# The last four quads of an attention block as 256 tokens of two heads each, with half of the last feed-forward moved forward

## The chip, the cores and the metric

One core of a Trainium2 chip runs the whole kernel. The metric is device time in microseconds of one execution, the median over runs; the profile is that of one execution. Five engines work side by side, each through its own queue in order: PE (TensorE, matrix products into PSUM), ACT (ScalarE), DVE (VectorE), POOL (GpSimd) and SP (SyncE, which here issues transfers). PSUM has eight banks of 128 x 512 floats.

## What is computed

A transformer block over 2048 tokens of width 512, with 32 heads of 16 and a feed-forward of width 1376. Six vectors sa, ca, ga, sb, cb, gb come from one conditioning vector:

```python
h = _layernorm(x, axis=-1) * (1 + ca) + sa
x = x + ga * _A_ref(h, A_wqkv, A_wo)
h = _layernorm(x, axis=-1) * (1 + cb) + sb
x = x + gb * _B_ref(h, B_w1, B_b1, B_w2, B_b2)
```

`_A_ref` is softmax attention with an output projection, `_B_ref` two matrix products with a GELU (tanh form) between them and biases. Inputs and outputs are bf16.

## The kernel before

**Tiling.** Queries go in four blocks `b` of 512 tokens (`NQB`), keys in sixteen tiles `kt` of 128 (`NKT`). Heads go in groups `ch` of eight; within a group the heads lie in pairs on four strips of 32 partitions, so that four heads of the same parity `par` are worked at once. Four heads, 512 queries and all keys are a *quad*; there are 32 (`NQ`), in the order of `divmod(qi, 8)`: block, group, parity (`bt`, L802). I count them from 0 to 31.

**A quad.** For each key tile and strip PE makes scores `S = kT.T qm` (L871, 32 x 128 weights, 512 columns, one of four row groups of the array). Most are turned into weights by ACT: one exponential (L1216) takes the scores of two strips, 1024 columns. The others go another way, "D": DVE rounds score plus constant into int16 (L1287), whose bits read as f16 are a power of two, and makes, with POOL, three shifted copies (L1258 on DVE, L1264 on POOL), which with scaled values `VV` approximate the exponential. PE then multiplies the weights by the values (L1027): 128 x 32 weights, 512 columns, four column groups of the array at once, one for each head. Each head's 32 output rows hold its 16 sums and, from a column of ones, the softmax denominator. All of a quad add up in one bank, which is opened by `open_o`.

**After a quad.** `o_copy` copies the bank to SBUF (L1321, DVE). SP then carries the four rows of denominators to DRAM and back into a 128 x 16 shape (`d`, `dall`, L1331 and L1340), DVE takes reciprocals (L1357), SP writes them out (L1365) and reads them back, repeated over 16 partitions (`rb`, L1375). For the odd quad the rows are merged into those of the even one (L1327). POOL multiplies (L1386) and leaves `OT[(b, ch)]`, 128 channels by 512 tokens. Quad 30 is a special one: its `OT` is made alone, and quad 31 is handled in the tail.

**Feed-forward of a block.** When a block's four `OT` are there, `add_tail(b)` gives jobs: x1 (projection by `W_o` and the residual), norm, transposes by DMA on SP, eleven "u" jobs (up-projection), one GELU on ACT over the whole, four "out" jobs. They are worked between the matmuls of the next block's quads.

**What sets the order.** A program written in Python (from L700) plans everything before the kernel runs: it keeps four clocks, picks at each step the next instruction of PE, ACT, DVE or POOL, and emits it. So the queues are fixed in advance. A job or a task has a gate (a place in the sequence of quads), things it depends on, and a planned duration: `MM` for a step on PE, `K_GATE`, `U_GATE`, `OUT_GATE` and so on for gates. When PE would be idle, `fill` adds four matmuls of zeros (L1042).

**The tail** (`last_tail`, from L1501). Once the loop is over, the sums of quad 31 lie in PSUM. x1 of the last block is nearly done by "z" jobs (residual and three groups, by 128 x 128 matmuls at L680). Then: copy (L1518), the denominators through `pick` (L1522), reciprocal (L1524), spread to rows (L1527, L1529), product (L1533), the last group's part of x1 with `W_z`, statistics (L1562), root on POOL (`ln_root`), the norm's scaling half on DVE and half on ACT (L1573, L1571), transposes on PE (L1580), the up-projection in slices of 256 tokens (`up_one`: four matmuls and a GELU, L1553), ten warming matmuls before it (`warm`, L251), the down-projection (L680), the residual sum and the store. All 512 tokens go through this chain after the loop.

Of the kernel before, what the change touches and what calls it, by code (L numbers as in the profile page):

```python
# [100 lines left out]
Z_AHEAD = 3  # L101
# [3 lines left out]
Z_GATE = 0.2  # L105
# [50 lines left out]
def adaln_block(ctx: ExitStack, tc: tile.TileContext, A_x, A_wqkv, A_wo, B_x, B_w1, B_b1, B_w2, B_b2,  # L156
# [254 lines left out]
    pick = const.tile([P, 4], FP32, name="pick")  # L411
    nc.vector.tensor_copy(out=pick, in_=ident32.rearrange("p (r e) -> p r e", e=32)[:, :, 14])
# [284 lines left out]
    def add_tail(b):  # L697
        X = {}
        def span(g, i, n):
# [3 lines left out]
             lambda: X.update(tail_tiles(b)), out=(SP_X, 512.0))  # L703
# [29 lines left out]

        for fc in range(NFC):
            job(("u", b, fc), span(U_GATE, fc, NFC), [("t2", b, t) for t in range(4)] + [("w1s", j) for j in range(NC)] + [("b1t", 2)],
                [lambda ps, j=j, fc=fc: up_mm(bank(ps), X["h2"], fc, j, mm=mm4) for j in range(NC)],
                [((DV,), lambda eng, ps, fc=fc: u_evac(ps, fc))])
        task(("g", b), span(U_GATE, NFC, NFC), [("u", b, fc) for fc in range(NFC)], AC, 7.5,
# [13 lines left out]
        for tt in range(4):  # L752
            job(("out", b, tt), span(OUT_GATE, tt, 4), [("g", b)] + [("w2g", fc) for fc in range(NFC)],
                [lambda ps, tt=tt, fc=fc: down_mm(bank(ps), X["u"], tt, fc, mm=mm4) for fc in range(NFC)],
                [((DV,), lambda eng, ps, tt=tt: o_evac(ps, tt))])
# [4 lines left out]

    def outer(ps, tt):
        b, cs = NQB - 1, slice(tt * P, (tt + 1) * P)
        return [lambda: plain(ps, ident, XL["xr"][:, tt, :], True, False)] + [
            lambda ch=ch: plain(ps, OT[(b, ch)][:, cs], W_o[:, ch, :], False, False) for ch in range(3)]

    for tt in range(Z_AHEAD):
        job(("z", tt), NQ - Z_GATE + 0.001 * tt, ["xlast"] + [("ot", NQB - 1, ch) for ch in range(3)],
            [lambda ps, tt=tt, i=i: outer(bank(ps), tt)[i]() for i in range(4)], [], mode="full")
    task("xlast", 8 * NQB - 0.9, [("out", NQB - 2, tt) for tt in range(4)], "SP", 0.0,
         lambda: XL.update(tail_tiles(NQB - 1)), out=(SP_X, 512.0))  # L770
# [30 lines left out]

    def bt(qi):  # L802
        b, t = divmod(qi, 8)
# [65 lines left out]
    def qk(dst, qi, kt, r):  # L869
        b, ch, par = bt(qi)  # L870
        nc.tensor.matmul(out=dst, lhsT=kT[32 * r:32 * r + 32, ch, kt * P:(kt + 1) * P],  # L871
                         rhs=qm[(b, ch)][32 * r:32 * r + 32, par, :], start=True, stop=True)
# [114 lines left out]
    def open_o(now):  # L987
        qi = opened[0]
        if qi < NQ and may_open(qi) and o_wait(now):
            f = flex_free(now)  # L990
            if f:
# [4 lines left out]
                left_q[qi] = 4  # L996

# [18 lines left out]
    def pv_issue(now, sel):  # L1016
        s = pe_start(now, "col", MM, "col" if len(sel) == 4 else f"part{len(sel)}")
        for r, e in sel:
# [3 lines left out]
            h = 8 * ch + 2 * r + par  # L1022
            lo = VOFF + HS * h - (16 if par else 0)
            w = VE[:, kt, lo:lo + 32] if not j else VV[:, DKT.index(kt), j - 1, lo:lo + 32]
            n = emitted[qi][r] + 1
            last = total(qi) == n
            nc.tensor.matmul(out=bank(O[qi])[32 * r:32 * r + 32, :], lhsT=w, rhs=rhs, start=(n == 1), stop=last)  # L1027
# [8 lines left out]
    def fill(now):  # L1036
        for qi in sorted(O):
            rs = [r for r in range(4) if emitted[qi][r] and emitted[qi][r] != total(qi)]
            if len(rs) == 4:
                pe_start(now, "col", MM, "fill")  # L1040
                for r in rs:
                    nc.tensor.matmul(out=bank(O[qi])[32 * r:32 * r + 32, :], lhsT=zeros[:, 0:32],  # L1042
                                     rhs=hT[:, r, 0:512], start=False, stop=False)
# [48 lines left out]
    def pe(now):  # L1092
        if issue_unit(now):
            return True
        open_o(now)
# [81 lines left out]
    def do_task(now, e, upto=INF):  # L1177
        p = min(pos(), upto)
        for tk in tasks:
            if tk.gate > p:  # L1180
                break
            if tk.eng == e and is_done(tk.deps, now):
                if e == "SP" and tk.name[0] in ("tb", "xlast") and now < chain[0]:
# [118 lines left out]
    def o_copy(now):  # L1302
        if not o_done or o_done[0][0] > now:
            return False
        if bt(o_done[0][1])[2] and o_done[0][1] < NQ - 1 and o1_free[0] > now:
            return False
# [5 lines left out]
        if par == 0:  # L1312
# [10 lines left out]
        row = 14 if par else 16  # L1323
        d1 = scr.tile([4, 512], FP32, name="d1")

        def merge(r):
            nc.sync.dma_start(out=o[32 * r + 16:32 * r + 32, :], in_=dst[32 * r + 16:32 * r + 32, :])  # L1327
            return dma(st["ev"], SP_O)

        def first():  # L1330
            nc.sync.dma_start(out=d1, in_=dst.rearrange("(r e) n -> r e n", e=32)[:, row, :])  # L1331
            land = dma(t, SP_D)
            st["ev"] = t
            if par:
                for r in range(2):
                    merge(r)
            at(land, lambda: second(land))

        def second(now):
# [3 lines left out]
            if par:  # L1343
# [5 lines left out]
        if par:  # L1349
# [11 lines left out]
        def after(now, rp):  # L1361
# [7 lines left out]
            def bq(now):  # L1369
                for r in range(4):  # L1370
                    lo = 32 * r + 16 * par
                    if qi == NQ - 2:
                        nc.sync.dma_start(out=rb[32 * r:32 * r + 32, :], in_=d2[r:r + 1, :].to_broadcast([32, 512]))
                    else:
                        nc.sync.dma_start(out=rb[lo:lo + 16, :], in_=d2[r:r + 1, :].to_broadcast([16, 512]))  # L1375
                    land = dma(now, SP_RB)
                chain[0] = land
                if par or qi == NQ - 2:
                    done[("rb", b, ch)] = land + DMA_SLACK

            at(now, a)
            if par or qi == NQ - 2:
                def mk():
                    ot = otp.tile([P, 512], BF16, name="OT")
                    OT[(b, ch)] = ot
                    nc.gpsimd.tensor_tensor(out=ot, in0=o, in1=rb, op=ALU.mult)  # L1386

                tasks.insert(0, Task(("ot", b, ch), -1, [("rb", b, ch)], PO, 1.42, mk))
# [62 lines left out]
    while more_units() or bulk or filled or dbanks or dcur[0] or shifts or any(queue) or O or len(jobs) or xopen or evacs:  # L1451
# [34 lines left out]
        else:  # L1486
            T[e] = now + 0.02
            guard += 1
            if guard > 40000:
# [12 lines left out]
    def last_tail():  # L1502
# [5 lines left out]
        rest = [i for i in range(8) if i != kO and i not in pz]  # L1508
        po, kw, kd, kr = pz + rest[0:4 - len(pz)], *rest[4 - len(pz):7 - len(pz)]
# [3 lines left out]
        rx = odp.tile([P, 512], FP32, name="rb")  # L1513

        def last_ch(tt):
            plain(bank(po[tt]), OT[(b, 3)][:, tt * P:(tt + 1) * P], W_z[:, 0, :], False, False)

        nc.vector.tensor_copy(out=o, in_=bank(kO))  # L1518
        for tt in range(len(pz)):
            last_ch(tt)  # L1520
        for tt in range(4):
            nc.tensor.matmul(out=bank(kd)[:, 4 * tt:4 * tt + 4], lhsT=o[:, tt * P:(tt + 1) * P], rhs=pick,  # L1522
                             start=True, stop=True)
        nc.vector.reciprocal(out=rt.rearrange("p t r -> p (t r)"), in_=bank(kd)[:, 0:16])  # L1524
        for tt in range(4):
            cs = slice(tt * P, (tt + 1) * P)
            nc.vector.tensor_copy(out=rx[:, cs].rearrange("p (r e) -> p r e", e=32),  # L1527
                                  in_=rt[:, tt, :].unsqueeze(2).to_broadcast([P, 4, 32]))
            nc.tensor.matmul(out=bank(kr)[:, cs], lhsT=rx[:, cs], rhs=ident32, start=True, stop=True)  # L1529
        nc.scalar.activation(out=onec, in_=onec, func=ACT.Gelu_apprx_tanh)  # L1530
        for h in range(2):
            cs = slice(256 * h, 256 * h + 256)
            nc.vector.tensor_tensor(out=otl[:, cs], in0=o[:, cs], in1=bank(kr)[:, cs], op=ALU.mult)  # L1533
        nc.sync.dma_start(out=scr_d1, in_=o.rearrange("(r e) n -> r e n", e=32)[:, 14, :])
        nc.sync.dma_start(out=dall[:, NQ - 1, :], in_=scr_d1.rearrange("r (p f) -> (r p) f", f=16))
        def last_par(tt):
            plain(bank(po[tt]), otl[:, tt * P:(tt + 1) * P], W_z[:, 1, :], False, True)

        for tt in range(2):
            last_par(tt)  # L1540
        for tt in range(len(pz), 4):
            for fn in outer(bank(po[tt]), tt):
                fn()
            last_ch(tt)
        for tt in range(2, 4):
            last_par(tt)
        warm(10, kw)

        def up_one(fc, cs, k):
            ps = bank(k)[:, 0:256]  # L1550
            for j in range(NC):
                up_mm(ps, h2, fc, j, cs)
# [214 lines left out]
```

## Time and profile before

| | |
|---|---|
| median of 3 runs | 757.46 us (756.5 to 757.7) |
| the profiled execution | 757.77 us, span of its trace 756.0 us |
| granted TensorE clock | 0.997 |
| exponentials, L1216 | 734 |
| score matmuls, L871 | 2048, of which 580 feed DVE's way |
| value matmuls, L1027 | 3788, in 947 groups of four |
| last scores of quad 31 begin | 719.31 us |
| the sums of quad 31 are copied | 721.59 us |
| first up-projection of the last block | 732.38 us |
| last down-projection ends | 752.53 us |

In the timeline a line is a run of like instructions: start, us, engine, line of the code, operation, output and inputs, shape, number, and in brackets how long the engine was idle before and who released it. In the table of groups the columns are busy time and mean length, and then the idle time before them. `32*128` is the part of the array that a matmul uses, rows by columns.

### The profile page before, as it was taken

Reading aid. Unit: us, or ns where it says so; the run is one execution under the profiler, and the core shown is the slowest. Engines: PE = TensorE matmul, PEld = TensorE weight load, DVE = VectorE, ACT = ScalarE, POOL = GpSimd, SP = SyncE. Lnnn points to the kernel's source line nnn. Section 1 sums busy time; section 2 is a strip of 40 time slices with the busy share of each in tenths; the row PEclk is TensorE's granted clock in tenths of the full one; section 3 lists DMA queues with packets and bytes.
Section 4 is the critical chain, followed back from the end, with each engine's and each line's share of the span. In section 5 each row is a group of like instructions: output and inputs, shape, how many; then the busy total and the mean of one; then the engine's idle time right before and its main releaser. Section 6 shows DMA issues by size and latency. Waiting matters only on the chain.

```text
span 756.0 us, 21028 instructions
## 1 busy us (share of the span) xinstructions
PE 738.0 (98%) x8528; PEld 229.1 (30%) x8528; DVE 686.2 (91%) x1196; ACT 720.7 (95%) x778; POOL 420.5 (56%) x264
## 2 busy tenths in 40 slices
PE   7999999999999999999999999999999999999998
PEld 3322322222233222222232222222222222222255
DVE  5958999999989999999999999999999999999942
ACT  3999999999999999999999999999999999999953
POOL 3202557666566753276659575765666656657510
PEclk9999999999999999999999999999999999999999
DMA  8410100021210110000100200001010200001100
GB/s 297 130 22 2 25 11 17 8 67 48 59 50 11 26 28 13 14 17 24 45 17 10 43 7 16 10 23 24 28 34 3 45 10 17 10 17 31 42 12 31
DMA packets 40248, 25.33 MB, mean 34 GB/s; under 512 B 25265, under 2 KB 34962, under 8 KB 40146
## 3 DMA queue, kind: packets, MB, share of 16 engines
q1 hardware_dynamic: 39186, 22.69, 11.7%
q8 instruction: 68, 1.11, 0.6%
q10 hardware_dynamic: 960, 1.25, 0.5%
q14 instruction: 34, 0.28, 0.1%
HBM read 16.72 MB, written 2.61 MB: 26 GB/s over the span
## 4 chain that ended last, share of the span: by engine, by line
ACT 49%; PE 37%; issue 8%; DVE 3%; POOL 2%; DMA 0%; POOLq 0%; DVEq 0%; ACTq 0%
ACT pB L1216 23%; ACT pA L1216 23%; PE PS L1027 13%; PE PS L871 12%; PE PS L246 7%; PE PS L680 3%; POOL t L1264 2%; ACT uG L739 1%; DVE t L1287 1%; PE PS L1042 1%; DVE t L1258 1%; DMA xb<-in_A_x_dram 0%; PE PS L251 0%; ACT L1216 0%; DVE st L273 0%
## 5 line engine op out<-in xcount | busy, mean ns | idle before, releaser
L1264 POOL TENSOR_SCALAR t<-t 128x2048 int16<-128x2048 int16 x189 | 358.0, 1901 | 250.9 <-DVE t L1258 130.1
L1216 ACT ACTIVATE pA<-PS 128x1024 bf16<-128x1024 f32 x367 | 391.8, 1068 | 3.7 <-PE PS L871 3.6
L1287 DVE TENSOR_SCALAR t<-PS 128x512 int16<-128x512 f32 x580 | 374.8, 680 | 21.5 <-PE PS L871 18.5
L1216 ACT ACTIVATE pB<-PS 128x1024 bf16<-128x1024 f32 x367 | 391.7, 1067 | 0.4 <-PE PS L871 0.2
L871 PE MATMUL PS<-qm,kT 32*128 32x512 bf16 x2048 | 308.2, 383 | 5.6 <-ACT pB L1216 1.9
L1027 PE MATMUL PS<-t,VV 128*32 128x512 f16 x1740 | 225.5, 385 | 3.2 <-POOL t L1264 2.7
L1258 DVE TENSOR_SCALAR t<-t 128x2048 int16<-128x2048 int16 x246 | 177.0, 743 | 0.4
L871 PEld LDWEIGHTS <-kT 32*128 32x128 bf16 x2048 | 85.6, 91 | 298.0 <-issue 295.3
L1027 PE MATMUL PS<-pA,VE 128*32 128x512 bf16 x734 | 166.8, 385 | 0.0
L1027 PE MATMUL PS<-pB,VE 128*32 128x512 bf16 x734 | 164.1, 386 | 0.0
L1027 PE MATMUL PS<-t,VE 128*32 128x512 f16 x580 | 141.8, 385 | 0.2 <-DVE t L1287 0.2
L1027 PEld LDWEIGHTS <-VE 128*32 128x32 bf16 x2048 | 61.8, 94 | 75.4 <-issue 68.8
L1027 PEld LDWEIGHTS <-VV 128*32 128x32 bf16 x1740 | 58.0, 94 | 64.2 <-issue 57.9
L246 PE MATMUL PS<-h2T,W 128*32 128x512 bf16 x528 | 42.6, 383 | 0.0
L246 PE MATMUL PS<-W,uG 128*32 128x512 bf16 x528 | 40.7, 383 | 0.0
L1386 POOL TENSOR_TENSOR OT<-o_sb,rb 128x512 bf16<-128x512 f32 x16 | 20.4, 1274 | 14.7 <-DVE t L1258 6.8
L1042 PE MATMUL PS<-hT,zeros 128*32 128x512 bf16 x284 | 28.3, 382 | 0.0
L731 DVE TENSOR_SCALAR uG<-PS,b1c 128x512 bf16<-128x512 f32 x33 | 24.5, 741 | 1.5 <-PE PS L246 1.5
L333 DVE TENSOR_SCALAR qm<-PS,qmask 128x512 bf16<-128x512 f32 x32 | 22.6, 741 | 3.5 <-PE PS L246 3.3
L283 POOL TENSOR_SCALAR rs<-mv 128x4 f32<-128x4 f32 (+1 forms) x10 | 4.5, 449 | 32.3 <-DVE mv L278 31.8
L246 PE MATMUL PS<-hT,W_k 128*32 128x512 bf16 x256 | 21.3, 398 | 0.9 <-DVE hT L316 0.9
L246 PE MATMUL PS<-hT,W_q 128*32 128x512 bf16 x256 | 21.3, 397 | 0.0
(133 smaller groups left out, 381.7 us busy)
## 6 DMA issues: line engine op xcount, KB each, us to landing
rb<-d SPq DMA_DIRECT2D x120, 32.0 KB
W_m<-in_w_mod_dram SPq DMA_DIRECT2D x2, 1024.0 KB
xr<-in_A_x_dram SPq DMA_DIRECT2D x4, 512.0 KB
o_sb<-o SPq DMA_DIRECT2D x60, 32.0 KB
out_dram<-ob SPq DMA_DIRECT2D x14, 128.0 KB
xb<-in_A_x_dram SPq DMA_DIRECT2D x3, 512.0 KB
W<-in_B_w_dram SPq DMA_DIRECT2D x4, 344.0 KB
W<-in_B_w_dram SPq DMA_DIRECT2D x5, 256.0 KB
```

The costliest lines, as they stand in the source:

```text
L246: nc.tensor.matmul(out=ps[32 * g:32 * g + 32, :], lhsT=lhsT[:, 32 * g:32 * g + 32], rhs=rhs, start=start, stop=stop)
L333: nc.vector.tensor_scalar(out=qm[(b, ch)][:, par, :], in0=ps, scalar1=qmask[:, par:par + 1], scalar2=None, op0=ALU.mult)
L680: nc.tensor.matmul(out=ps, lhsT=lhsT, rhs=rhs, start=start, stop=stop)
L731: nc.vector.tensor_scalar(out=X["u"][:, fc, :], in0=bank(ps), scalar1=late["b1c"][:, fc:fc + 1], scalar2=None, op0=ALU.add)
L871: nc.tensor.matmul(out=dst, lhsT=kT[32 * r:32 * r + 32, ch, kt * P:(kt + 1) * P], rhs=qm[(b, ch)][32 * r:32 * r + 32, par, :], start=True, ...
L1027: nc.tensor.matmul(out=bank(O[qi])[32 * r:32 * r + 32, :], lhsT=w, rhs=rhs, start=(n == 1), stop=last)
L1042: nc.tensor.matmul(out=bank(O[qi])[32 * r:32 * r + 32, :], lhsT=zeros[:, 0:32], rhs=hT[:, r, 0:512], start=False, stop=False)
L1216: nc.scalar.activation(out=t[:, 0:n, :], in_=PS[:, b0:b0 + n, :], func=ACT.Exp, scale=math.log(2.0) / STEP)
L1258: nc.vector.tensor_scalar(out=t16[:, rs, :], in0=d["tile"][:, rs, :], scalar1=float(MJ[j]), scalar2=None, op0=ALU.add)
L1264: nc.gpsimd.tensor_scalar(out=t16[:, rs, :], in0=d["tile"][:, rs, :], scalar1=1.0, scalar2=float(MJ[j]), op0=ALU.mult, op1=ALU.add)
L1287: nc.vector.tensor_scalar(out=d["tile"][:, r:r + n, :], in0=PS[:, i:i + n, :], scalar1=T_BIAS, scalar2=0.0, op0=ALU.add, op1=ALU.max)
L1386: nc.gpsimd.tensor_tensor(out=ot, in0=o, in1=rb, op=ALU.mult)
```

## The change

Six things are changed.

1. The last four quads are cut otherwise. They are still those of block 3, groups 2 and 3, but each now holds 256 tokens of *both* parities: quad 28 is group 2, first half; 29 group 3, first half; 30 and 31 the second half. A score matmul still has 512 columns (two parities of 256). A value matmul becomes two of 256 columns, one for each parity, with different weights into the same strip. The bank is opened by four matmuls of zeros.
2. `o_copy` follows: two transfers of denominators in place of one, four merges within the quad's own tile, eight broadcasts of 256, and an `OT` of 256 tokens for each of these quads but the last.
3. x1, statistics and norm of the *first* 256 tokens of the last block become jobs and tasks of the loop (`add_half`, gate `XA_AT`), with the norm's scaling on POOL and the transposes by DMA. They lie in parts of `hT` that nothing reads any more (`xa`, `ha`, `ua`); filler matmuls read `kT` for that reason, and the path for out-of-range inputs, which is not run with these inputs, computes again what it took from `hT`.
4. In the tail only the second 256 tokens go through the chain. The first half's up- and down-projection are steps of a generator, and `gap(n)` issues n of them at six places of the chain (`GAPS`). The ten warming matmuls go.
5. "z" jobs, now two, are for the second half alone; the x load is in two parts.
6. Gates: `K_GATE`, `U_GATE`, `OUT_GATE`, `Z_GATE`, `OPEN_N`, and own ones for block 2.

The core of the diff:

```diff
-K_GATE = (-1.7, 0.25)
+K_GATE = (-1.7, 0.22)
-U_GATE = (1.7, 5.0)
-OUT_GATE = (4.6, 7.8)
-OPEN_N = 14
+U_GATE = (2.2, 5.2)
+OUT_GATE = (5.0, 7.9)
+OPEN_N = 12
-Z_AHEAD = 3
+GAPS = (4, 2, 2, 17, 2, 3)
+NHQ = 4
+N2_ENG = PO
+NHC = NC - NHQ // 2
+MMH = 0.25
+XA_AT = 30.5
+U2_GATE = (1.7, 4.6)
+OUT2_GATE = (4.6, 7.2)
-Z_GATE = 0.2
+Z_GATE = 0.6
...
+    def halved(qi):
+        return qi >= NQ - NHQ
+
     def bt(qi):
+        if halved(qi):
+            h, n = divmod(qi - NQ + NHQ, NHQ // 2)
+            return NQB - 1, NHC + n, h
...
+                if halved(qi):
+                    pe_start(now, "col", MM, "opens")
+                    for r in range(4):
+                        nc.tensor.matmul(out=bank(f[0])[32 * r:32 * r + 32, :], lhsT=zeros[:, 0:32], rhs=zeros,
+                                         start=True, stop=False)
+                    return True
...
         for r, e in sel:
...
+            for pr in range(2) if halved(qi) else (par,):
+                lo = VOFF + HS * (8 * ch + 2 * r + pr) - (16 if pr else 0)
+                w = VE[:, kt, lo:lo + 32] if not j else VV[:, DKT.index(kt), j - 1, lo:lo + 32]
+                cs = slice(256 * pr, 256 * pr + 256) if halved(qi) else slice(0, 512)
+                nc.tensor.matmul(out=bank(O[qi])[32 * r:32 * r + 32, cs], lhsT=w, rhs=rhs[:, cs],
+                                 start=(n == 1 and not halved(qi)),
+                                 stop=last and (pr == 1 or not halved(qi)))
...
+        for tt in range(2):
+            job(("xA", tt), XA_AT, ["xl0"] + [ot_key(ch, 0) for ch in range(NC)],
+                [lambda ps, tt=tt, ch=ch: mm4(bank(ps), ot_cols(ch, tt), W_o[:, ch, :], ch == 0, ch == NC - 1)
+                 for ch in range(NC)],
+                [((DV,), lambda eng, ps, tt=tt: x1(ps, tt))])
+            task(("s2", b, tt), XA_AT, [("xA", tt)], DV, 0.64, lambda tt=tt: ln_stats(xa, XL["st"], tt))
+        task(("a2", b), XA_AT, [("s2", b, tt) for tt in range(2)], DV, 0.3,
+             lambda: XL.update(mv=ln_aggr(XL["st"][:, 0:2, :], 2)))
+        task(("r2", b), XA_AT, [("a2", b)], PO, 1.2, lambda: XL.update(rs=ln_root(XL["mv"], 2)))
+        def n2(tt):
+            hn.append(otp.tile([P, 512], BF16, name="OT"))
+            eng = nc.vector if N2_ENG == DV else nc.gpsimd
+            eng.tensor_scalar(out=hn[tt], in0=xa[:, tt, :], scalar1=XL["mv"][:, tt, 0:1],
+                                    scalar2=XL["rs"][:, tt:tt + 1], op0=ALU.subtract, op1=ALU.mult)
+        for tt in range(2):
+            task(("n2", b, tt), XA_AT, [("r2", b)] + [("n2", b, 0)] * tt, N2_ENG, 0.36 if N2_ENG == DV else 0.55,
+                 lambda tt=tt: n2(tt))
+            task(("t2", b, tt), XA_AT, [("n2", b, tt)], "SP", 0.0,
+                 lambda t=tt: transpose_dma(ha[:, :, t * P:(t + 1) * P], hn[t]), out=(SP_T, 0.0))
...
+                for r in range(4):
+                    for i in range(2) if half else (par,):
+                        lo = 32 * r + 16 * i
+                        nc.sync.dma_start(out=rb[lo:lo + 16, 0:w], in_=d2[r:r + 1, cs].to_broadcast([16, w]))
...
+        def fillers():
+            for fc in range(NFC):
+                up_one(fc, (kw, dA[1])[fc % 2], 0)
+                for _ in range(2):
+                    yield
+            for tt in range(2):
+                for fc in range(NFC):
+                    plain(bank(dA[tt]), ua(fc)[:, tt * P:(tt + 1) * P], late["W_2"][:, fc, :], fc == 0, fc == NFC - 1)
+                    yield
...
         nc.vector.tensor_copy(out=o, in_=bank(kO))
+        nc.scalar.activation(out=onec, in_=onec, func=ACT.Gelu_apprx_tanh)
+        gap(GAPS[0])
...
-        warm(10, kw)
```

The tail after that goes on: `pick` (four matmuls), reciprocal, `gap(2)`, the spread to rows, `gap(2)`, the two products and the last parts of x1 of two token tiles, statistics and root, `gap(17)`, the norm's scaling (one tile on ACT, one on DVE), transposes, `gap(2)`, four slices of the second half's up-projection, the rest of the generator, seven more slices, the flag, and the down-projection of the second half.

More of the change, by code (lines that the diff above doesn't have):

```diff
@@ L1513, in last_tail, with up_one @@
         rx = odp.tile([P, 512], FP32, name="rb")
[L1515 to L1522, printed above, removed]
+        hA, hB = slice(0, 256), slice(256, 512)
+        obs = {}
+        def up_one(fc, k, half):
+            ps = bank(k)[:, 0:256]
+            for j in range(NC):
+                up_mm(ps, h2 if half else ha, fc, j, hB if half else hA)
+            nc.scalar.activation(out=uG[:, fc, hB] if half else ua(fc), in_=ps, func=ACT.Gelu_apprx_tanh, bias=b1c[:, fc:fc + 1],
+                                 scale=1.0)
```

290 lines of the change are left out of this document (160 added, 130 removed).

## The prediction

> **What bounds the kernel now.** I read the page first: busy shares and the chain of waits.
>
> ```profile
> PE 738.0 (98%) x8528; PEld 229.1 (30%) x8528; DVE 686.2 (91%) x1196; ACT 720.7 (95%) x778; POOL 420.5 (56%) x264
> ACT 49%; PE 37%; issue 8%; DVE 3%; POOL 2%; DMA 0%; POOLq 0%; DVEq 0%; ACTq 0%
> L1216 ACT ACTIVATE pA<-PS 128x1024 bf16<-128x1024 f32 x367 | 391.8, 1068 | 3.7 <-PE PS L871 3.6
> ```
>
> Up to 721 us the exponentials (L1216) and TensorE set the time together: ACT carries 49% of the chain, PE 37%. Exponentials start 0.907 us apart when nothing holds them (the 1068 ns of a row overlap). Second, the timeline of the last 40 us:
>
> ```profile
> 719.31 0.39 PE L871 MATMUL PS<-qm,kT 32*128 32x512 bf16 x2
> 720.07 0.38 PE L1027 MATMUL PS<-pB,VE 128*32 128x512 bf16 x2
> 720.28 0.60 PE L1027 MATMUL PS<-t,VV 128*32 128x512 f16 x8
> 721.59 0.69 DVE L1518 COPY o_sb<-PS 128x512 f32<-128x512 f32 x1 [2.31 <-PE PS L1027]
> 723.64 0.95 PE L1522 MATMUL PS<-pick,o_sb 128*128 128x4 f32 x8
> 732.38 3.22 PE L680 MATMUL PS<-h2T,W 128*128 128x256 bf16 x28 [0.45 <-ACT h2T L324]
> 742.62 7.30 PE L680 MATMUL PS<-W,uG 128*128 128x512 bf16 x33
> 752.57 0.37 ACT L324 CAST ob<-PS 128x256 bf16<-128x256 f32 x1 [9.47 <-PE PS L680]
> ```
>
> The last scores start at 719.31, the last quad's sums are copied at 721.59, and until 732.38, 10.8 us, PE mostly waits for a chain of small steps (denominators, x1, norm, transposes). Then 20.2 us of dense feed-forward run to 752.53; the span ends at 756.0. The change wants to put half of that feed-forward into the 10.8 us. Third, what its input would have to come through: the chain of the last but one quad ("quad 30"), DVE and then everything, and two POOL rows:
>
> ```profile
> 705.26 0.68 DVE L1321 COPY o_sb<-PS 128x512 f32<-128x512 f32 x1
> 707.29 1.87 DVE L1287 TENSOR_SCALAR t<-PS 128x512 int16<-128x512 f32 x3
> ```
> ```profile
> 714.90 0.23 DVE L1357 RECIPROCAL rp<-dall 128x16 f32<-128x16 f32 x1
> 715.17 0.32 SPq L1365 DMA_DIRECT2D d<-rp  x1
> 716.20 3.08 DVE L1258 TENSOR_SCALAR t<-t 128x2048 int16<-128x2048 int16 x5
> 716.61 2.61 SPq L1373 DMA_DIRECT2D rb<-d  x4
> 721.09 1.27 POOL L1386 TENSOR_TENSOR OT<-o_sb,rb 128x512 bf16<-128x512 f32 x1 [6.44 <-DMA rb<-d]
> ```
> ```profile
> L1264 POOL TENSOR_SCALAR t<-t 128x2048 int16<-128x2048 int16 x189 | 358.0, 1901 | 250.9 <-DVE t L1258 130.1 <-PE PS L871 39.3 <-DVE t L1287 27.4
> L577 POOL TENSOR_SCALAR W_z<-W_o,pmask 128x512 bf16<-128x512 bf16 x2 | 3.1, 1574 | 0.6 <-DVE o_sb L1321 0.6
> ```
>
> From its copy to its scaled output quad 30 takes 705.26 to 722.36, longer than the loop still runs.
>
> **The change, part by part**, against this execution (span 756.0, its own time 757.77; the median of the runs is 757.46).
>
> (1) *The loop, amounts.* By the two built programs' orders there are 736 exponentials for 734, 576 passes L1287 for 580, 244 DVE shifts for 246, 71 filler groups in both. For PE I price every step of the order by starts in this trace: 0.2175 us for a group of four 128x32 matmuls (720.07 to 720.28, and on), 0.314 where the array changes between row and column tiles, 0.2175 for a 128x128 one. That gives 667.6 before. The last four quads now take their 124 value groups as eight 256-wide matmuls. No row shows such a group; 256-wide matmuls at L680 stand 0.112 apart (6.71 for 60), so two per column group in turn are 0.224 from below. From above: if the eight ran column after column, four steps of 0.107, 0.43. I take 0.23, because in this trace a matmul of a free column group does not wait for one whose column is busy:
>
> ```profile
> 240.47 0.39 PE L1027 MATMUL PS<-pA,VE 128*32 128x512 bf16 x2
> 240.48 0.59 PE L246 MATMUL PS<-W_o,OT 128*32 128x512 bf16 x4
> ```
>
> The pair at 240.47 holds column groups 0 and 1. Of the four behind it two start 0.01 later and two at 240.69; the records at 240.69 are those with the wait on DVE, which the program gives to the first of the four. So groups 2 and 3 went first. With 0.23 PE's price is 667.8 (three groups more for x1, four zero openings, fewer tile changes elsewhere): +0.2. ACT's is two exponentials, 2 x 0.907 = +1.8. Both bind in turn, so the loop's end moves by +0.2 to +1.8; I take +0.6, nearer PE, whose order loses fewer steps in the quads before. With 0.43 per group PE's price is +25.
>
> [...]
>
> (2) *Quad 30's chain and the first half's norm.* This sets my end. Take as zero the scores of the exponential before which the last two passes ahead of quad 30's copy are fed; 15 exponentials follow, so the last scores stand at 15 x 0.93 = 13.95 (0.93 is the pace of these quads with their small waits: 23 in 21.4 us in quad 31). DVE then has: pass, copy, two more passes, an x1 add and a stats, three passes, a shift (passes 0.60 apart, 707.29) and reaches the reciprocal at 6.8. From there by the rows above: 0.27 to d, 1.44 to rb, eight broadcasts instead of four at 0.43 (1.72 for four of 16 rows) 3.44, landing 1.87 (719.22 to 721.09), OT half as wide 0.66: 14.5. Behind OT in POOL's queue stand the two new norm steps (128x512 bf16, two operands by partition). No row has them: L1264 per element gives 0.475, L577 gives 1.57; I take L577, the same type and form: 17.7. Then SP, behind the broadcasts, the second transpose: 1.20 to issue (the minimum of the rows of L504) and 1.35 to land (eight early ones were issued by 41.28, the reader L316 started at 42.64): 20.3.
>
> Meanwhile PE: DVE's last shift ends at 15.7 (seven shifts at 0.61 behind two further passes' work, x1, stats and three passes); the last value group waits for it, then eight 128x128 matmuls of the last x1 (1.74), two array changes and the last pair: copy of the last sums at 18.75. PE's queue now has two feed-forward slices of the first half *before* the denominators; they need the transposes of 20.3, so PE stands 1.6 us, and pick, reciprocal, x1, norm, all queued behind them, stand with it.
>
> (3) *The tail.* Removed: 10 warming matmuls (2.32 at L251), one half's x1, stats, norm, transposes and copies. Moved into gaps: 11 slices of 4 matmuls, 22 down matmuls. From the first slice: slices 0.9; pick 0.2 + 0.95; reciprocal, four copies and the four products L1529 (from the end of L1522 to that of L1529) 1.85; one slice 0.45; last products 0.9; stats, root on POOL 2.7. PE fills with seven slices; they alternate two banks, each free again 1.17 after its slice begins (0.64 to the GELU, 0.43, 0.1), so 0.585 each, and the last GELU ends 9.9 after the first slice. The norm's ACT half is queued behind those GELUs (0.78); 1.07 from it to the first slice of the second half (731.31 to 732.38): 11.7. Left then: 44 matmuls x 0.112, 28 x 0.2205, a flag 0.25, and 2.97 (749.54 to 752.53) as before: 14.3. To the end 3.47 as before. Sum 29.5 from the first slice; before, from 719.31, the end was 36.7 away.
>
> (4) *At nothing*: new DMA issues (third copy of d, 4 merges instead of 2+2, 12 broadcasts more over three quads; SP stands idle most of the stretch; uncovered, 0.43 each in the chain of (2), where I counted the four that matter), the x load in two halves, the general path (not taken), other gates.
>
> *Sum*: old last scores 719.31 + 0.6 - 13.95 + 20.35 + 29.5 = 755.8 against 756.0: -0.2. On the median, 757.46 - 0.2 = 757.3.
>
> **The rivals.**
>
> *Faster: the input is there in time.* If POOL's norm steps go at 0.475 the transposes land at 18.1, PE waits only for the shifts (first slice at 18.7, -1.65), and if DVE runs ahead so that the last copy follows the last scores by 3.5, another -1.3. For it: L1264's rate, and DVE idle 2.31 before the last copy now. Against: both bf16 rows of POOL. 757.3 - 1.65 = 755.6 to 754.4; I give 755.0.
>
> *Slower: quad 30's chain drags.* Its place is the first slice, ahead of pick in PE's queue. Now copy to OT's end takes 17.1; with 0.83 for more broadcasts, 0.5 for a second d, 0.6 less in OT, it is 17.8 after 1.06, 18.9; norm and transpose 5.8: 24.7, which is 4.4 later than 20.3. For it: the reciprocal's 9 us behind the copy now; against: fewer steps stand between them. 757.3 + 4.4 = 761.7. It decides once the transposes land more than 1.6 us later than I say.
>
> *Slower: column groups in turn.* If a busy column group holds those behind it, a value group takes 0.43, PE's price rises by 25, of which the idle of these quads, some 5 us, hides a part: 757.3 + 20 = 777. For it no row; against it those at 240.48. [...]
>
> **How the numbers follow.** What a measurement of this kernel can tell from no change is about 0.2%, 1.5 us. Forecast (within that) 0.36; faster 0.35; dragging chain 0.23; columns in turn 0.06. So faster 0.35, same 0.36, slower 0.29. Likeliest: 757.3, its own range 755.9 to 759.0. The range for 8 in 10 reaches both neighbours, 753.5 (both gains of the faster case and 0.9 more) to 761.8, and leaves out the columns in turn.
>
> **What would show it.** Eight value matmuls starting within 0.24 us, not 0.43; PE idle before the first slice after the last value matmul, released by the transposes; L577-like 1.5 us for the two POOL norm steps; seven slices some 0.58 apart; then 14 us without a gap. I am wrong if the first slice follows the last value matmul at once, if those quads take over 24 us each without GELU, or if the second half's first slice starts much before 11 us after the first slice.

## The result, and the profile after

The changed kernel takes 760.95 us (median; 760.4 to 761.81), the kernel before 757.7 us beside it (756.5 to 757.97). The ratio is 1.0045 with a 95% interval of 1.003 to 1.006: slower by 0.45%, clear of noise. The forecast was 757.3. The number belongs to the rival "quad 30's chain drags" (761.7), and so does the place. But 3.2 us, as much as the whole loss, came from something that no case of the prediction had.

The page of the changed kernel: busy times, shares of the chain, and one half of the exponentials.

```profile
PE 737.3 (97%) x9027; PEld 241.3 (32%) x9030; DVE 679.7 (90%) x1189; ACT 719.7 (95%) x777; POOL 421.7 (56%) x266
PE 44%; ACT 43%; issue 8%; POOL 2%; DVE 1%; DMA 1%; POOLq 0%; ACTq 0%
L1300 ACT ACTIVATE pA<-PS 128x1024 bf16<-128x1024 f32 x368 | 395.1, 1074 | 3.4 <-PE PS L944 3.3
```

Nothing in the busy times shows a loss; the loop is bound as before. In this profile the span is 759.2 us against 756.0. The last scores (L944) start at 718.82, 0.5 us *sooner* than before. The profiles of this study differ by up to 1.6 us in when the first scores start: those whose clock stood at one half for 3.41 us just before (11.34 to 14.76 us in the kernel before) start at 15.5 to 16.0 us, the others at 14.3 to 14.6. So from here on stretches are compared: from the first scores to the last 703.1 us (703.4 before), and from the last scores to the end 40.4 us (36.7 before). The whole loss is in the tail. The timeline:

```profile
703.56 0.41 PE L1108 MATMUL PS<-t,VV 128*32 128x256 f16 x8
703.79 0.40 PE L1108 MATMUL PS<-t,VE 128*32 128x256 f16 x8
...
722.11 0.40 PE L1108 MATMUL PS<-pB,VE 128*32 128x256 bf16 x4
722.55 0.69 DVE L1639 COPY o_sb<-PS 128x512 f32<-128x512 f32 x1 [3.21 <-PE PS L1108]
726.80 1.89 PE L689 MATMUL PS<-hT,W 128*128 128x256 bf16 x8 [4.30 <-DMA hT<-OT]
728.49 1.71 PE L1644 MATMUL PS<-pick,o_sb 128*128 128x4 f32 x8
730.05 1.01 PE L689 MATMUL PS<-hT,W 128*128 128x256 bf16 x4
730.97 2.08 PE L1651 MATMUL PS<-ident,rb 128*128 128x128 f32 x8
735.36 4.08 PE L689 MATMUL PS<-hT,W 128*128 128x256 bf16 x28
741.69 1.91 PE L689 MATMUL PS<-h2T,W 128*128 128x256 bf16 x16
754.35 1.36 PE L689 MATMUL PS<-W,uG 128*128 128x256 bf16 x11
```

The reader is to see three things. Eight value matmuls take 0.23 us (703.56 to 703.79). The first two slices, ahead of `pick`, wait 4.30 us for the transposes `hT<-OT`. And after that wait everything on PE is slow: eight matmuls of 256 columns take 1.69 us (726.80 to 728.49, 0.21 each; 0.112 at L680 before), `pick` takes 1.71 us where it took 0.95. From the first slice to the second half's first slice (741.69) 14.9 us pass. Windows of half a microsecond tell why; the column before the last two is the granted clock:

```profile
core 0: us, PE busy (x) PEld busy (x) DVE busy (x) ACT busy (x) POOL busy (x), PEclk, DMA share, GB/s
724.50:725.00 0.50, 0.00 (x0) 0.00 (x0) 0.00 (x0) 0.00 (x0) 0.00 (x0) 1.00 0.00 0
725.00:725.50 0.50, 0.00 (x0) 0.00 (x0) 0.00 (x0) 0.00 (x0) 0.00 (x0) 0.55 0.00 0
725.50:726.00 0.50, 0.00 (x0) 0.00 (x0) 0.00 (x0) 0.00 (x0) 0.00 (x0) 0.50 1.00 193
...
735.00:735.50 0.50, 0.50 (x4) 0.27 (x3) 0.50 (x1) 0.00 (x0) 0.00 (x0) 0.71 0.00 0
735.50:736.00 0.50, 0.50 (x7) 0.46 (x5) 0.45 (x2) 0.00 (x1) 0.00 (x0) 1.00 0.00 0
```

Some 2.5 us into the wait TensorE's clock drops to half, and it stays there for 10.2 us, through all the small steps of the chain. All five runs have a mean granted clock of 0.991, so this profile is not an exception; of the 25 runs of the kernel before beside e1 to e4, 24 have 0.997 to 1.000. In the kernel before PE never stood longer than 0.7 us in this stretch, and its clock was 1.00 throughout. Last, why the transposes were late:

```profile
704.06 0.68 DVE L1407 COPY o_sb<-PS 128x512 f32<-128x512 f32 x1
710.41 0.24 DVE L1456 RECIPROCAL rp<-dall 128x16 f32<-128x16 f32 x1
712.12 4.20 SPq L1474 DMA_DIRECT2D rb<-d  x8
715.07 4.28 DVE L1342 TENSOR_SCALAR t<-t 128x2048 int16<-128x2048 int16 x7
715.24 1.13 POOL L291 TENSOR_SCALAR rs<-mv 128x2 f32<-128x2 f32 x1 [0.64 <-DVE mv L286]
716.46 1.12 POOL L292 TENSOR_TENSOR rs<-rs,mhalf 128x2 f32<-128x2 f32 x1
719.43 0.73 POOL L1486 TENSOR_TENSOR OT<-o_sb,rb 128x256 bf16<-128x256 f32 x1 [1.85 <-DVE t L1342]
720.15 4.15 POOL L804 TENSOR_SCALAR OT<-hT,mv,rs 128x512 bf16<-128x512 bf16 x2
722.26 3.26 SPq L513 DMA_TRANSPOSE hT<-OT  x2
```

It is the chain of the forecast, step for step, with one wait that the forecast does not have. The root of the norm is ready on POOL at 717.6 (its last step, L292, runs from 716.46 for 1.12 us), but the two norm steps (L804) stand in the queue behind `OT` of quad 30, and that starts only at 719.43; then they take 2.08 us each.

`OT` does not wait for its broadcasts: the trace's records of their landing end at 717.52. The row names DVE's shifts (L1342), the last of which ends at 719.35, 0.08 us before `OT` starts. By the rows of e1 to e3 and e5 to e8, 0.07 to 0.09 us stand between DVE's last shift and `OT` of quad 30; in e4 no shift runs at that time. The two steps of the root (L291, L292), too, run beside the shifts, and take 1.13 and 1.12 us; in this profile's tail, with no shift beside them, they take 0.23 and 0.73. `OT` reads nothing that a shift writes; what couples POOL to DVE here was not taken apart by a run.

### The profile page after: what moved, and what is told of

It is laid out like the page before. It is cut to its first block, busy times and chain, and to the rows that moved or that the text cites. A ratio compares the mean times of both kernels' runs of the same rounds, so it can differ in the third digit from the quotient of the medians.

```text
span 759.2 us, 22066 instructions
## 1 busy us (share of the span) xinstructions
PE 737.3 (97%) x9027; PEld 241.3 (32%) x9030; DVE 679.7 (90%) x1189; ACT 719.7 (95%) x777; POOL 421.7 (56%) x266
## 3 DMA queue, kind: packets, MB, share of 16 engines
q1 hardware_dynamic: 41042, 23.02, 11.7%
q10 hardware_dynamic: 816, 1.12, 0.4%
## 4 chain that ended last, share of the span: by engine, by line
PE 44%; ACT 43%; issue 8%; POOL 2%; DVE 1%; DMA 1%; POOLq 0%; ACTq 0%
ACT pB L1300 21%; ACT pA L1300 21%; PE PS L1108 15%; PE PS L944 15%; PE PS L254 10%; PE PS L689 2%; ACT uG L749 1%; POOL t L1348 1%; POOL OT L804 1%; DMA xb<-in_A_x_dram 0%; DVE st L281 0%; PE PS L1125 0%; DVE t L1371 0%; ACT uG L1620 0%; ACT L1300 0%
## 5 line engine op out<-in xcount | busy, mean ns | idle before, releaser
L1348 POOL TENSOR_SCALAR t<-t 128x2048 int16<-128x2048 int16 x188 | 355.7, 1901 | 257.6 <-DVE t L1342 149.7
L944 PE MATMUL PS<-qm,kT 32*128 32x512 bf16 x2048 | 306.8, 383 | 6.5 <-ACT pA L1300 2.7
L1108 PE MATMUL PS<-t,VV 128*32 128x512 f16 (+1 forms) x1968 | 228.6, 358 | 2.5 <-POOL t L1348 1.4
L944 PEld LDWEIGHTS <-kT 32*128 32x128 bf16 x2048 | 85.1, 91 | 288.6 <-issue 285.5
L1342 DVE TENSOR_SCALAR t<-t 128x2048 int16<-128x2048 int16 x244 | 174.2, 743 | 0.5
L1108 PE MATMUL PS<-pA,VE 128*32 128x512 bf16 (+1 forms) x824 | 170.2, 362 | 0.0
L1108 PE MATMUL PS<-pB,VE 128*32 128x512 bf16 (+1 forms) x824 | 165.7, 362 | 0.0
L1108 PE MATMUL PS<-t,VE 128*32 128x512 f16 (+1 forms) x656 | 134.6, 358 | 0.2 <-DVE t L1371 0.2
L1108 PEld LDWEIGHTS <-VE 128*32 128x32 bf16 x2304 | 70.0, 94 | 76.6 <-issue 70.3
L1108 PEld LDWEIGHTS <-VV 128*32 128x32 bf16 x1968 | 65.4, 95 | 55.6 <-issue 51.1
L1125 PE MATMUL PS<-kT,zeros 128*32 128x512 bf16 x284 | 27.4, 383 | 0.0
L291 POOL TENSOR_SCALAR rs<-mv 128x4 f32<-128x4 f32 (+1 forms) x10 | 4.3, 433 | 37.4 <-DVE mv L286 37.3
L1486 POOL TENSOR_TENSOR OT<-o_sb,rb 128x512 bf16<-128x512 f32 (+1 forms) x17 | 20.0, 1179 | 9.0 <-DVE t L1342 7.6
```

Source lines behind the costliest of these rows:

```text
L944: nc.tensor.matmul(out=dst, lhsT=kT[rows, ch, kt * P:(kt + 1) * P], rhs=rhs, start=True, stop=True)
L1108: nc.tensor.matmul(out=bank(O[qi])[32 * r:32 * r + 32, cs], lhsT=w, rhs=rhs[:, cs], start=(n == 1 and not halved(qi)), stop=last and (pr = ...
L1342: nc.vector.tensor_scalar(out=t16[:, rs, :], in0=d["tile"][:, rs, :], scalar1=float(MJ[j]), scalar2=None, op0=ALU.add)
L1348: nc.gpsimd.tensor_scalar(out=t16[:, rs, :], in0=d["tile"][:, rs, :], scalar1=1.0, scalar2=float(MJ[j]), op0=ALU.mult, op1=ALU.add)
L1486: nc.gpsimd.tensor_tensor(out=ot[:, 0:w], in0=o[:, 0:w], in1=rb[:, 0:w], op=ALU.mult)
```

## The experiments

Stretches are those of each run's profile, in us: from the first scores to the last; from the last scores to the first slice of the first half; from there to the first slice of the second half; from the last scores to the end. The last column is the median of the runs, with their bounds.

| | loop | to first slice | to second half | last scores to end | runs |
|---|---|---|---|---|---|
| before | 703.4 | - | - | 36.7 | 757.7 (756.5 to 757.97) |
| changed | 703.1 | 7.98 | 14.89 | 40.4 | 760.95 (760.4 to 761.81) |
| e1: zeros in the wait, 20 | 703.4 | 7.98 | 11.66 | 37.2 | 757.83 (756.74 to 760.5) |
| e2: norm on DVE | 703.5 | 4.09 | 11.55 | 33.1 | 752.8 (752.78 to 752.92) |
| e3: slices behind the products | 703.1 | 10.76 | 5.81 | 37.8 | 757.26 (754.95 to 759.75) |
| e4: old gates | 705.8 | 5.54 | 11.66 | 34.7 | 758.66 (756.95 to 759.13) |
| e5: zeros, 8 | 705.9 | 8.0 | 14.1 | 39.6 | 758.79 (757.23 to 761.84) |
| e6: e2 and e3 | 703.2 | 8.4 | 5.2 | 35.0 | 754.65 (754.14 to 755.5) |
| e7: e2, three banks | 703.2 | 4.1 | 10.7 | 32.3 | 751.71 (751.67 to 752.87) |
| e8: e7, fewer slices ahead of the norm | 703.5 | 4.1 | 10.2 | 32.9 | 753.14 (752.54 to 754.25) |
| e9: before, new gates | 702.0 | - | - | 37.3 | 757.65 (755.21 to 759.22) |
| e10: e7, down matmuls behind the norm | 707.7 | 4.1 | 10.7 | 33.1 | 753.04 (752.17 to 757.18) |

**e1: keep PE busy in the wait.**

```diff
         nc.scalar.activation(out=onec, in_=onec, func=ACT.Gelu_apprx_tanh)
+        warm(20, kw)
         gap(GAPS[0])
```

> The changed kernel, with twenty 128x128 by 512 matmuls of zeros into the bank `kw` put in PE's queue between the copy of the last sums and the first feed-forward slice of the first half (20 x 0.2175 us = 4.35 us, about the 4.3 us that PE stood there). The transposes still land when they did, so the first slice still starts some 8 us after the last scores. Theory (the wait for the transposes let the granted clock fall to 0.50, and the chain after it ran at half clock): the clock stays 1.00, the time from the first slice to the second half's first slice falls from 14.9 us to the forecast 11.7, the span from 759.2 to about 756.0, and the runs come out at about 757.7. Rival (the chain of small steps was underestimated whatever the clock): that stretch stays at 14.9 us and the span at 759.2.

The timeline of this run:

```profile
722.78 4.49 PE L259 MATMUL PS<-zeros 128*128 128x512 bf16 x20
727.14 1.05 PE L689 MATMUL PS<-hT,W 128*128 128x256 bf16 x8
728.02 0.95 PE L1645 MATMUL PS<-pick,o_sb 128*128 128x4 f32 x8
...
738.80 1.91 PE L689 MATMUL PS<-h2T,W 128*128 128x256 bf16 x16
```

The first slice starts as long after the last scores as without the zeros (7.98 us), but runs at 0.11 us per matmul, `pick` takes 0.95, and the second half's first slice follows after 11.66 us (forecast: 11.7). The zeros compute nothing and take 3.2 us off the tail. The theory holds: of the tail's 40.4 us the clock made 3.2, and the chain of small steps had been sized rightly. The runs come out at 757.83, where 757.7 was expected; one of the ten took 760.5 us at a mean clock of 0.993, and where its clock fell is not known.

**e2: the norm of the first half on DVE.**

```diff
-N2_ENG = PO
+N2_ENG = DV
```

> The changed kernel with the two norm steps of the first half on DVE in place of POOL (N2_ENG = DV); they stand in DVE's queue behind three and four of the last seven shifts. Nothing else of the loop's queues moves. Theory (the first slices wait for POOL's two steps of 2.08 us, behind OT of quad 30): the transposes land at about 721.7 us, before the copy of the last sums; DVE's last shifts and that copy come at most 1.2 us later; the wait before the first slice (4.3 us) goes, and with it the half clock; first slice at 723.3 to 724, second half's first slice 11.7 later, span 752.5 to 753.5, which is 2.5 to 3.5 below the kernel before. Rival (the transposes are late for SP or the DMAs, or the chain drags elsewhere): the first slice stays within 1 us of 726.8 and the span at 757 or more.

The timeline of this run:

```profile
716.50 0.41 DVE L804 TENSOR_SCALAR OT<-hT,mv,rs 128x512 bf16<-128x512 bf16 x1 [0.61 <-POOL rs L292]
716.95 2.66 SPq L513 DMA_TRANSPOSE hT<-OT  x2
717.43 0.41 DVE L804 TENSOR_SCALAR OT<-hT,mv,rs 128x512 bf16<-128x512 bf16 x1
717.75 1.90 DVE L1342 TENSOR_SCALAR t<-t 128x2048 int16<-128x2048 int16 x3
719.73 0.73 POOL L1486 TENSOR_TENSOR OT<-o_sb,rb 128x256 bf16<-128x256 f32 x1 [3.26 <-DVE t L1342]
720.38 0.69 DVE L1639 COPY o_sb<-PS 128x512 f32<-128x512 f32 x1 [0.73 <-PE PS L1108]
722.00 1.04 PE L689 MATMUL PS<-hT,W 128*128 128x256 bf16 x8
733.55 1.91 PE L689 MATMUL PS<-h2T,W 128*128 128x256 bf16 x16
```

The two steps take 0.41 us each (2.08 on POOL), no longer stand behind `OT` (which waits for DVE's last shift until 719.73 here), and are done at 717.84. The first slice waits for nothing but PE's own queue, starts 3.9 us sooner after the last scores, and the clock stays at 1.00. The tail falls by 7.3 us to 33.1, 3.6 less than before the change: 3.9 from the first slice and 3.3 from the stretch behind it, of which the clock is 3.2 by e1. Against the expectation, PE's last steps did move: the planner now puts the eight "z" matmuls of the second half behind the last value group, not ahead, so the copy comes 2.5 us after the last scores, not 3.7. What share that has in the 3.9 was not tried by itself. The ratio to the kernel before is 0.9939 (0.9923 to 0.9956): one constant turns the change from a loss of 0.45% into a gain of 0.6%. Not all of that gain lies in the tail: of the 5.0 us between the spans of this profile and of the kernel before 3.6 are the tail and 1.4 the earlier first scores (14.45 us against 15.88), with which the constant has nothing to do.

**e3: leave the input late, put the slices elsewhere.**

```diff
-GAPS = (4, 2, 2, 17, 2, 3)
+GAPS = (0, 0, 0, 10, 2, 3)
```

> The changed kernel with the gaps (0, 0, 0, 10, 2, 3): no slice of the first half stands ahead of pick, the spread or the products; five follow the last products, one follows the norm's transposes, the rest stand behind four slices of the second half. The transposes land as late as before (726.8). Theory (the place of the first slices, ahead of pick in PE's queue, turns a late input into a late chain): pick starts some 1.1 us after the copy of the last sums, at 723.6; the second half's first slice at about 733.4 (10.8 us after the copy, as in the kernel before); the clock stays at 1.00, as in that kernel, whose PE has the same small pieces of work there; span about 754.3, that is 4.9 below the changed kernel and 1.7 below the kernel before. Rival (with PE mostly idle for 4 us the clock falls all the same, or slices crowd the norm): second half's first slice at 736 or later and span 757 or more.

The timeline and two windows of this run:

```profile
723.32 1.05 PE L1644 MATMUL PS<-pick,o_sb 128*128 128x4 f32 x8 [0.79 <-DVE o_sb L1639]
735.40 1.91 PE L689 MATMUL PS<-h2T,W 128*128 128x256 bf16 x16
```
```profile
724.50:725.00 0.50, 0.00 (x0) 0.00 (x0) 0.36 (x2) 0.00 (x0) 0.00 (x0) 0.65 0.00 0
731.00:731.50 0.50, 0.50 (x4) 0.33 (x3) 0.00 (x0) 0.22 (x1) 0.42 (x2) 0.52 0.00 0
```

`pick` starts early, as the theory had it, but in this execution the clock still fell at 724.65 (from the mean of the first window) and came back at 731.5; the second half's first slice came at 735.4, nearer to the rival's 736 than to the theory's 733.4. The ten runs spread from 754.95 to 759.75, where those of e2 lie within 0.14. The three fastest (754.95 to 755.33, spans of 753.2 to 753.5) have a mean clock of 1.00, the four slowest (758.43 to 759.75) 0.990 to 0.993. So both hold in part: where the clock stays, the theory's span of 754.3 is reached and passed, and in the four slowest it does not stay. That the stops of 0.8 us between small pieces of work are what puts it at risk rests on this one profile. The kernel before has more matmuls in that place, and its longest stop is 0.7 us.

**e4: the old gates.** Six constants back (`K_GATE`, `U_GATE`, `OUT_GATE`, `OPEN_N`, and block 2's).

> The changed kernel with the gates of the kernel before (K_GATE, U_GATE, OUT_GATE, OPEN_N, and block 2's the same as the others'); the tail is that of the changed kernel. The built program has 738 exponentials in place of 736 and 572 passes on DVE in place of 576. Theory (the loop's end, 0.5 us earlier than in the kernel before, was held there by the retuned gates): last scores 1 to 3 us later than 718.8, tail unchanged but for the wait (the transposes fall with the last quads), span 760 to 762. Rival (the gates are worth nothing): span within 0.7 us of 759.2.

The timeline of this run:

```profile
720.51 4.15 POOL L804 TENSOR_SCALAR OT<-hT,mv,rs 128x512 bf16<-128x512 bf16 x2
724.63 0.73 POOL L1486 TENSOR_TENSOR OT<-o_sb,rb 128x256 bf16<-128x256 f32 x1
727.36 1.05 PE L689 MATMUL PS<-hT,W 128*128 128x256 bf16 x8 [0.70 <-DMA hT<-OT]
```

Both theories missed: the loop is 2.7 us longer, as the first one said, yet the run is 2.3 us *faster* than the changed kernel. The lines suggest why. The plan falls otherwise, and on POOL the two norm steps now stand *ahead* of `OT` of quad 30. They are as slow as before, but PE waits 0.70 us in place of 4.30, the clock stays at 1.00, and the tail is 5.7 us shorter. It goes with e1 and e2, where PE did not stand long in this place (0.54 and 0.53 us at most up to the second half's first slice) and the clock stayed at 1.00. The run agrees with `OT`'s place in POOL's queue being a part of the delay, but does not show it by itself, since DVE's shifts end earlier too (719.2, 2.6 us before the last scores) and the root's two steps take 0.23 and 0.72 us here.

**e5: eight zeros in place of twenty.**

> As the run with twenty matmuls of zeros, with eight: PE is busy for 1.74 us of the wait for the transposes and stands for some 2.6 us. Theory (only a longer stretch with little work lets the granted clock fall; 4.3 us did, three stops of 0.5 to 0.7 us did not): the clock stays 1.00 in the profile, the time from the last scores to the end is that of the run with twenty, 37.2 us. Rival (a stop of 2.6 us is enough): the clock falls to 0.50 for some 8 us and the time from the last scores to the end is 39 to 40.4 us. With the edge between, runs of both kinds, 3 us apart.

The timeline and windows of this run:

```profile
728.46 1.41 PE L689 MATMUL PS<-hT,W 128*128 128x256 bf16 x8 [2.46 <-DMA hT<-OT]
```
```profile
728.50:729.00 0.50, 0.50 (x5) 0.45 (x6) 0.00 (x0) 0.00 (x0) 0.00 (x0) 1.00 0.01 2
729.00:729.50 0.50, 0.50 (x5) 0.36 (x4) 0.00 (x0) 0.33 (x1) 0.00 (x0) 0.50 0.03 8
```

A stop of 2.46 us was enough here: PE was at work again when, half a microsecond later, the clock went to 0.50 until 735.8. That is the rival in this execution. The runs lie between 757.23 and 761.84, with mean clocks from 0.997 in the three fastest to 0.991 in the slowest, so the outcome is not the same each time. (This profile's loop lost 2.8 us in quad 9, which has no part in the tail. There the clock stood at one half from 234.07 to 240.89 us, although PE had no stop above 0.3 us around it; so one fall in one profile does not prove what made it.)

**e6: input in time and slices behind the products.** e2 and e3 together.

> Norm steps on DVE and the gaps (0, 0, 0, 10, 2, 3): the input is in time, and the first slices still stand behind the products. Theory (what the early slices are worth is PE's busy time in the small steps, which holds the clock): from the last scores to the end 34 to 36 us, against 33.1 with the slices ahead of pick, more where the clock falls in the small steps, and runs of more than one kind. Rival (the slices ahead of pick only delay the chain by their own 0.9 us each time): 31.5 to 32.5 us.

The tail is 35.0 us, within the theory's range and 1.9 more than e2; the rival falls. But the clock was 1.00 here from 720 to 738, so its reason was wrong in this execution: what is lost is PE's time in the small steps, which the early slices would have filled.

**e7: three banks for the first half's slices.**

```diff
-                up_one(fc, (kw, dA[1])[fc % 2], 0)
+                up_one(fc, (kw, dA[1], dA[0])[fc % 3], 0)
```

> Norm steps on DVE, and the slices of the first half go round three banks (kw, dA[1], dA[0]) in place of two. Theory (two banks hold the slices at 0.585 us, and the norm's ACT half stands behind their GELUs): the seven slices of the fourth gap start 0.45 us apart, the second half's first slice 0.8 us sooner after the first slice (10.75 in place of 11.55), last scores to end 32.3 us in place of 33.1. Rival (ACT sets the slices' pace, or PE is packed anyway): under 0.2 us of gain.

The seven slices of the fourth gap in the timelines of e2, and then of e7:

```profile
727.22 4.08 PE L689 MATMUL PS<-hT,W 128*128 128x256 bf16 x28
```
```profile
726.83 3.22 PE L689 MATMUL PS<-hT,W 128*128 128x256 bf16 x28
```

The slices fall from 0.58 to 0.45 us, the second half follows the first slice after 10.68 us, and the tail takes 32.3 us, each as expected. This is the fastest kernel of the study: 751.71 us, ratio to the kernel before 0.9934 (0.9917 to 0.995).

**e8 and e10: other shares of work ahead of the norm**, `GAPS` (4, 2, 2, 11, 2, 3) and (4, 2, 2, 14, 2, 3) on e7.

> As the run with three banks, with the gaps (4, 2, 2, 11, 2, 3): six slices in place of seven and three down matmuls fewer ahead of the norm. Theory (the GELUs ahead of the norm's ACT half set the second half's first slice): last scores to end 31.9 us. Rival (work taken from the gap comes back behind it): within 0.2 us of the run with seven slices.

> Norm steps on DVE, three banks, gaps (4, 2, 2, 14, 2, 3): seven slices ahead of the norm, as in the run with (4, 2, 2, 17, 2, 3), but the three down matmuls behind the transposes. Theory (the norm's ACT half follows the seventh GELU either way, so the down matmuls fill a stop of PE that is there anyway): PE stands 0.6 us more before the transposes and the same three matmuls come later, last scores to end 32.9 to 33.0 us against 32.3. Rival (they delay the transposes): 32.3 or less.

e8 misses: the second half did start 0.44 us sooner, but the tail is 32.9 us, not 31.9. The slice and the down matmuls taken out come back later on an engine that has no gap left, as the rival had it; but that costs 0.6 us, more than its 0.2. e10, 33.1 us, is close to what its theory said. (Its profile has a first quad 4.5 us longer than the others', with the clock at one half from 24.16 to 34.40 us; the tail is not touched by that.) What stands ahead of the norm fills a stop that is there anyway.

**e9: the new gates without the rest**, four constants in the kernel before.

> The kernel before with the changed K_GATE, U_GATE, OUT_GATE and OPEN_N alone; quads, tail and x1 as before. From the first scores to the last the loop took 703.4 us before, 703.1 in the changed kernel and 705.8 in the changed kernel with the old gates. Theory (the gates only pay back what the halved quads and the first half's x1 cost the loop, which the old gates leave at 2.4 us): with whole quads they gain under 0.7 us, loop 702.7 to 704, runs within 0.2% of the kernel before. Rival (the gates shorten any loop): loop 700.5 to 701.5, runs 2 us or more faster than the kernel before, and the halved quads cost 2 to 3 us under either set.

Neither: the loop is 1.5 us shorter in the profile (701.96), the tail 0.6 longer, and the runs are level with the kernel before (ratio 1.0005, 0.9993 to 1.0017). So the halved quads and the first half's x1 cost the loop 1.2 us under the new gates (703.1 less 702.0) and 2.4 under the old ones (705.8 less 703.4), by one profile each. Block 2's own gates, which e9 does not have, are in the first of these differences.

## Why the prediction was wrong

Seen from 755.8, the end that its sum gave for this profile, the span of 759.2 is 3.4 us too long. The steps, in its own order:

- *(1) The loop.* Last scores were forecast 0.6 us later and came 0.5 sooner: -1.1 (0.2 of it lie ahead of the first scores). The price of 0.23 for a value group is right to the digit, and the rival of column groups in turn falls (0.43 per group, an estimate that no run shows; 777 us). The amounts were sized rightly too: 1.2 us under the new gates, in the range of 0.2 to 1.8. The slip is in (4): "other gates" at nothing. By one profile each they take 1.5 us off the loop with whole quads and 2.7 with halved ones.
- *(2) The input's time.* Right place, right queue order, right order of steps; sizes off, and one wait left out. Counted from 13.95 us before the last scores, the reciprocal came at 5.5 (forecast 6.8), and then: the eight broadcasts took 4.20 us to issue (3.44) and landed 1.2 us after the last issue (1.87), `OT` then stood 1.9 us more until DVE's last shift was over (not in the sum), two norm steps on POOL took 4.15 (3.14), `OT` and the transposes were as forecast to 0.1. In sum the transposes landed 1.6 us later than said, at 21.9 in place of 20.3. At the same time DVE and PE were quicker than I allowed: the last copy came at 17.7, not 18.75. Both errors go the same way: a wait of 4.3 us in place of 1.6. Taking L577 over L1264's per-element price for POOL was the right choice between the two, and the truth lay beyond it: 2.08, above the larger of my two prices, 1.57 (L577 multiplies by one operand per partition, L804 subtracts one and multiplies by a second).
- *(3) The tail: the step that failed.* I booked a stop of PE at its length and nothing more, and so made 29.5 us from the first slice; it took 32.4. The 11.7 us to the second half's first slice are right at full clock (11.66 in e1, 11.55 in e2), the 14.3 and 3.47 behind it as well (14.0 and 3.5 measured). What was missing is that this wait let the clock fall to one half for what came after: 3.2 us, as e1 shows by filling the wait. All the rows I priced the chain from had been taken at a clock of 1.00, and I had read that clock in the windows of before without asking what kept it there. My reading that PE "mostly waits" in the 10.8 us of before was wrong, too: its stops there add up to 1.6 us, and the rest is "z" matmuls, the small products, transposes and 2.3 us of zeros.
- *The rivals.* "Quad 30's chain drags" named the place, and had 0.23. That its time was nearly right is luck: it had `OT` end 4.4 us later than forecast, and `OT` ended 0.8 later (15.3 in place of 14.5). It put a wait of 6.0 us there (4.4 more than the forecast's 1.6) and nothing behind it; measured are a wait of 4.3 and 3.2 us of half clock behind it, with the loop's last scores 1.1 us sooner than forecast. "Faster" would have needed POOL at 0.475 us per norm step; e2 shows that it was there for the taking on DVE at 0.41.

The sum: -1.1 from the loop, +1.6 from the late transposes, +3.2 from the clock and -0.3 from the dense part behind (14.0 in place of 14.3) make +3.4, the whole miss.

## What to carry to other kernels

Work moved into the gaps of a chain stands in the same queue as the chain: its input has to be there with room to spare, or it turns a filled gap into a wait, and everything behind it is late as well. Before pricing a wait on TensorE, ask what its clock will do: here a stop of 4.3 us cost 3.2 us more behind it, and one of 2.5 us 2.4 (14.1 in place of 11.66, e5). Twenty matmuls of zeros, or work whose input was there in time, kept the clock; eight did not in the profiled run. And price an operation moved to another engine by its own row there; the same norm step was 0.41 us on DVE and 2.08 on POOL. Ask also what the other engines run beside it: here POOL's `OT` stood until DVE's shifts were over.

## What the runs showed of the hardware

- The half clock came in portions. In the changed kernel it fell at 725.05 and rose at 735.29 (from the means 0.55 and 0.71 of the windows), 10.24 us; in e3 724.65 to 731.48, 6.83 us; in e5 729.0 to 735.83, 6.83 us. That is 3, 2 and 2 times 3.41; the one at the start of the kernel before and of the changed kernel lasted 3.41 (the traces of these two record 3.413, and 10.240 for the long one of the changed kernel). From the rise at 15.08 us to the fall at 725.05 in the changed kernel 709.97 us pass, 208.0 times 3.413. The clock fell 2.5 us into a stop of 4.30 us (the changed kernel), half a microsecond after a stop of 2.46 us with work on both sides (e5) and after pieces of work with stops of 0.8 us (e3); in e6, with stops of the same kind in the same places, the tail stays at 1.00. In the 3.41 us ahead of the fall PE was busy for 0.9 us in the changed kernel and 1.0 in e5, but for 2.3 us in e3, and in the loop of e5 and the first quad of e10 the clock fell with PE at work. What decides between them stays open.
- POOL's price for one operation is not one number: 128x512 bf16 with two operands by partition took 2.08 us (L804), 128x512 bf16 at L577 1.57, and a quarter of a shift at L1348, as many elements, 0.475 (1.90 / 4).
- Two operations of POOL came late or took longer beside DVE's shifts (L1342: 128x2048 int16 in and out). `OT` of quad 30 started 0.07 to 0.09 us after the last shift in eight profiles (the changed kernel, e1 to e3, e5 to e8), in the changed kernel 1.9 us after the last record of its broadcasts' landing, and the root's steps took 1.13 and 1.12 us beside shifts there, 0.23 and 0.73 without.
